# A Nyström attention and two-layer feed-forward kernel: the first stretch of the first layer written out as one fixed order for three engines

## The chip, the cores and the metric

The kernel runs on one core of a Trainium2 chip. The metric is device time in microseconds (us) of one execution. The kernel before took 865.08 us (median of three runs, 864.27 to 865.76).

## The reference, cut to what matters

Four images (batch entries) of 576 tokens go through Nyström attention with eight heads of width 64, then through two feed-forward layers.

```
q_lm, k_lm = block means of q, k over 18 tokens     # 32 landmarks
A  = softmax(q  @ k_lm.T * scale)                   # 576 x 32
Bm = softmax(q_lm @ k_lm.T * scale)                 # 32 x 32
C  = softmax(q_lm @ k.T * scale)                    # 32 x 576
Z  = Bm.T / (norm1(Bm) * norminf(Bm) + 1e-6)
for _ in range(6): Z = 2*Z - Z @ Bm @ Z
x  = A @ Z @ C @ v                                  # heads side by side: 2304 x 512
x  = ((x @ w_a) * (x @ w_b)) @ w_out                # first layer, 1536 wide
h  = x @ w_in;  out = (h * tanh(softplus(h))) @ w_out2   # second layer, 2048 wide, Mish
```

The weights arrive as 64-bit floats and are rebuilt as 32-bit ones on the chip.

## The kernel before, in words

**Attention of one image** is a list of steps: `kl` and `ql` (landmark sums on VectorE), `sB` and `BB` (the small softmax and its norms), six `NS` (the inverse), `sC0`, `sC1`, `ET0`, `ET1`, `U` (scores of the landmarks against k, their transposes, the product with v), `M` (inverse times U), and `A0`, `A1` with `A0n`, `A1n` (the left softmax in two halves of the tokens). Each step takes its PSUM from a pair of banks, tagged `at` or `bm`.

**Units** rebuild the weights. One unit is a DMA into a stage buffer (`stg`, three of them, and eight more at the start), an `Abs` on ScalarE (L317), and four VectorE instructions (L320 to L325). A unit of `w_out` has a split into a high and a low part as well (L334). Units 0 to 7 make `wab` of groups 0 and 1, units 8 to 11 four tiles `wo`, and so on up to 36.

**Folding** (`emit_bm`) multiplies `M` into `wab` and splits the result (`bm`). A **slot** (`emit_ab`) is then 12 matmuls into two banks `ps_ab`, a copy `ta` on ScalarE, a product `tg` on VectorE, and a split into `g` by ScalarE and GpSimd. Slots number 0 to 95, eight to a cell of one image and one third of the width: slots 0 to 7 are image 0, slots 8 to 15 image 1. An **output unit** (`emit_o1`) is 12 matmuls from four `g` and four `wo` into a bank `ps_o`, with an eviction into `x2acc`. `fill` issues matmuls of the identity that nobody reads.

**What sets the order.** Instructions of ScalarE and TensorE go through `Written` and keep the program's order as long as `Written.on` holds, which ends after step `A1` of image 0. Most of VectorE is free: a scheduler places its instructions by a simulated timeline. From slot 0 on a list `todo` says beside which slot each step of images 1 to 3 and each unit is emitted, and the scheduler orders the rest. SyncE issues all DMAs in one order, each when its buffer is free.

Before slot 56 the activation table for Mish is preloaded (L638); the exponentials of image 3 that come later load their own again.

Of the kernel before, what the change touches and what calls it, by code (L numbers as in the profile page):

```python
# [8 lines left out]
F32 = mybir.dt.float32  # L9
# [22 lines left out]
def nystrom_moe_kernel(ctx: ExitStack, tc: tile.TileContext, q, k, v, w_a, w_b, w_out1, w_in2, w_out2, out):  # L32
    nc = tc.nc
    NT = B * S
    ve, gp = nc.vector, nc.gpsimd

    class Written:
# [79 lines left out]

    def attention(ap, b, kt, qt, vt0=None):
# [3 lines left out]
        wheel = [0]  # L122
# [26 lines left out]
        def sB():  # L149
            p = pair()  # L150
            tile4(p, lambda o, rows, j: (o[:, 0:32], x["ql"][rows, j, :], x["kl"][rows, j, :]))
            st = x["st"] = sm([128, 2, 8], "stB")
            eb = sm([128, 2, LM], "eb")
            ve.tensor_reduce(out=st[:, :, 0], in_=p[:, :, 0:32], axis=AX, op=ALU.max)
            ve.tensor_tensor(eb, p[:, :, 0:32], st[:, :, 0:1].to_broadcast([128, 2, LM]), op=ALU.subtract)
            ac.activation(eb, eb, AF.Exp, scale=SC_B)
            ve.tensor_reduce(out=st[:, :, 2], in_=eb, axis=AX, op=ALU.add)
# [7 lines left out]
        def BB():  # L165

            st, bc = x["st"], x["bc"]
            p = pair()
            for c in range(2):
# [12 lines left out]
            ve.tensor_tensor(rz[:, :, 0], p[:, :, 64:96], rc, op=ALU.mult)  # L182
            ve.tensor_tensor(rz[:, :, 0], ist2, rz[:, :, 0], op=ALU.subtract)
            ve.tensor_tensor(rz[:, :, 1], bc[:, :, 0], rc, op=ALU.mult)
            x["n"] = 0

        def NS():
# [4 lines left out]
            p = pair()  # L192
            nx = x["rz"] = sm([128, 2, 2, LM], "rz", 2)
            for c in range(2):
                for h in range(4):
                    r = slice(32 * h, 32 * h + 32)
                    pe.matmul(
                        p[r, c, 32 * lo:64], rz[r, c, 0], rz[r, c, lo:2].rearrange("p a l -> p (a l)"),
                        start=True, stop=True,
                    )  # L200
            if not lo:
                ac.activation(nx[:, :, 0], p[:, :, 0:32], AF.Copy)
            ve.tensor_tensor(nx[:, :, 1], p[:, :, 32:64], rz[:, :, 1], op=ALU.add)
# [33 lines left out]
        def Uv():  # L237
            p = pair()
            for c in range(2):
                for i in range(5):  # L240
                    r = slice(0, min(128, S - 128 * i))
                    for j in range(4):
# [4 lines left out]
                        if (c, i, j) == (0, 0, 0):  # L247
                            tc.keep_in_program_order(ins)
# [6 lines left out]
        def M():  # L255
            p = pair()
            for c in range(2):
                pe.matmul(p[64 * c:64 * c + 64, 0, 0:128], x["U"][:, c], x["zd"][:, c].rearrange("p h l -> p (h l)"), start=True, stop=True)
            MT[b] = main.tile([128, 128], F32, tag="mt", bufs=3, name="mt")
            ac.activation(MT[b], p[:, 0, 0:128], AF.Copy)  # L260

        def A(r):
            p = pair()
# [3 lines left out]
            sa = x["sa"][:, r]  # L267
            for c in range(2):
                ve.transpose(out=sa[:, c], in_=p[:, c, 0:288])
            sa3 = sa.rearrange("p c (n l) -> p (c n) l", l=LM)  # L270
            ss = x["ss", r] = sm([128, 18, 4], "stA", 2)
            ve.tensor_reduce(out=ss[:, :, 0], in_=sa3, axis=AX, op=ALU.max)
            ve.tensor_tensor(sa3, sa3, ss[:, :, 0:1].to_broadcast([128, 18, LM]), op=ALU.subtract)
            ac.activation(sa, sa, AF.Exp, scale=SC_A)

        def An(r):
            ss, sa = x["ss", r], x["sa"][:, r]
            sa3 = sa.rearrange("p c (n l) -> p (c n) l", l=LM)
            ve.tensor_reduce(out=ss[:, :, 1], in_=sa3, axis=AX, op=ALU.add)
            ve.tensor_scalar(ss[:, :, 2], ss[:, :, 1], 1e-9, None, op0=ALU.add)  # L280
# [588 lines left out]
```

## Time and profile before

| | |
|---|---|
| median of three runs | 865.08 us |
| profiled execution, its own time | 862.38 us |
| its span, first to last instruction | 860.6 us |
| TensorE matmul busy | 805.4 us, 94% of the span |
| VectorE busy | 553.3 us, 64% |
| ScalarE busy | 346.1 us, 40% |
| GpSimd busy | 157.0 us, 18% |
| chain that ended last | PE 79%, DVE 12%, DMA 5% |

In the profile PE is TensorE's matmuls, DVE is VectorE, ACT is ScalarE, POOL is GpSimd, SP is SyncE. [...] A busy time is the time in which at least one instruction of the engine ran. The profiled run lies 2.7 us below the median.

### The profile page before, as it was taken

How to read it: one execution, taken by the hardware profiler on the slowest of the kernel's cores; microseconds unless marked ns; L12 is line 12 of the kernel's file. 1: busy time of each engine (PE TensorE's matmuls, PEld its weight loads, DVE VectorE, ACT ScalarE, POOL GpSimd, SP SyncE). 2: the span in 40 equal slices, each digit the busy share in tenths (PEclk: the TensorE clock that was granted, in tenths of full speed). 3: DMA queues.
4: the chain of work that ended last, by engine and by line, in shares of the span. 5: the costliest groups of instructions: out<-in, count | busy, mean ns of one | idle time of the engine just before them, and what ended most of it. 6: DMA issues, size and time to landing. Idle time of an engine off the chain costs nothing.

```text
span 860.6 us, 14629 instructions
## 1 busy us (share of the span) xinstructions
PE 805.4 (94%) x5830; PEld 696.0 (81%) x5830; DVE 553.3 (64%) x1024; ACT 346.1 (40%) x686; POOL 157.0 (18%) x147
## 2 busy tenths in 40 slices
PE   4767799999999999999898899999999999999998
PEld 3445578887897797887798799898989888998986
DVE  7787868888375379787996667858533347432433
ACT  3234436435332464353444545445323235332332
POOL 0022211222122133121226433521000000000000
PEclk9778699999999999999999999999999999999999
DMA  9532746649543816877576976789755446655502
GB/s 356 239 117 99 254 151 200 226 152 319 197 156 114 308 34 221 292 226 266 175 235 250 346 249 216 269 293 339 296 185 201 158 180 219 212 204 194 184 1 75
DMA packets 47605, 180.87 MB, mean 210 GB/s; under 512 B 4144, under 2 KB 12336, under 8 KB 37936
## 3 DMA queue, kind: packets, MB, share of 16 engines
q1 hardware_dynamic: 47536, 179.93, 58.8%
q8 instruction: 46, 0.75, 0.3%
q14 instruction: 23, 0.19, 0.1%
HBM read 126.44 MB, written 53.48 MB: 209 GB/s over the span
## 4 chain that ended last, share of the span: by engine, by line
PE 79%; DVE 12%; DMA 5%; issue 2%; ACT 1%; POOL 1%; SPq 0%; DVEq 0%; ACTq 0%
PE ps_ab L49 34%; PE ps_o L49 22%; PE ps_bm L49 13%; PE ps_at L49 10%; DVE f L324 1%; DMA wi2d<-f 1%; DVE f L325 1%; DVE f L320 1%; DMA qt<-in_q_dram 1%; DVE tg L437 1%; DMA kt<-in_k_dram 1%; DVE f L323 1%; DMA wo2d<-f 1%; DMA xq<-x2d 1%; DVE ql L138 1%
## 5 line engine op out<-in xcount | busy, mean ns | idle before, releaser
L49 PE MATMUL ps_ab<-xc,wc 128*128 128x384 f32 x1008 | 201.9, 339 | 2.6 <-ACT m L49 2.1
L49 PEld LDWEIGHTS ps_ab<-xc,wc 128*128 128x128 f32 x1008 | 181.6, 189 | 15.1 <-ACT m L49 2.3
L49 PE MATMUL ps_ab<-at,bm 128*128 128x288 f32 x1152 | 187.1, 303 | 6.9 <-DVE tg L437 4.3
L49 PEld LDWEIGHTS ps_ab<-at,bm 128*128 128x128 f32 x1152 | 161.3, 190 | 37.6 <-issue 9.8
L49 PE MATMUL ps_o<-g,wo 128*128 128x288 f32 x1152 | 182.2, 300 | 10.1 <-ACT wo L49 4.3
L49 PEld LDWEIGHTS ps_o<-g,wo 128*128 128x128 f32 x1152 | 162.6, 190 | 23.9 <-issue 7.3
L334 POOL TENSOR_TENSOR g<-tg,g 128x288 fp32r<-128x288 f32 x96 | 88.1, 918 | 283.6 <-ACT g L49 283.6
L49 ACT ACTIVATE m<-c 128x384 f32<-128x384 f32 x96 | 50.4, 525 | 185.5 <-DVE c L759 185.5
L49 PE MATMUL ps_bm<-wo,g 128*128 128x512 f32 x288 | 94.1, 394 | 0.3 <-ACT g L49 0.3
L49 PE MATMUL ps_at<-wo,g 128*128 128x512 f32 x288 | 83.3, 393 | 0.0
L49 PE MATMUL ps_o<-wo,g 128*128 128x512 f32 x288 | 79.4, 393 | 0.0
L49 ACT ACTIVATE g<-tg 128x288 fp32r<-128x288 f32 x96 | 42.6, 444 | 86.7 <-DVE tg L437 86.6
L334 DVE TENSOR_TENSOR g<-m,g 128x384 fp32r<-128x384 f32 x96 | 60.7, 633 | 25.8 <-ACT g L49 25.7
L437 DVE TENSOR_TENSOR tg<-ps_ab,ta 128x288 f32<-128x288 f32 x96 | 43.4, 452 | 30.3 <-PE ps_ab L49 24.3
L49 PEld LDWEIGHTS ps_at<-wo,g 128*128 128x128 f32 x288 | 53.9, 188 | 10.3
L49 PEld LDWEIGHTS ps_o<-wo,g 128*128 128x128 f32 x288 | 53.6, 188 | 8.9
L49 PEld LDWEIGHTS ps_bm<-wo,g 128*128 128x128 f32 x288 | 53.4, 187 | 7.0 <-ACT g L49 0.6
L49 ACT ACTIVATE ta<-ps_ab 128x288 f32<-128x288 f32 x96 | 38.9, 405 | 44.0 <-PE ps_ab L49 43.6
L49 ACT ACTIVATE g<-m 128x384 fp32r<-128x384 f32 x96 | 50.6, 527 | 2.9
L759 DVE TENSOR_TENSOR c<-ps_ab,m 128x384 f32<-128x384 f32 x24 | 13.4, 557 | 51.8 <-PE ps_ab L49 51.8
L49 PE MATMUL ps_bm<-wab,mt 64*32 64x512 f32 x384 | 42.2, 636 | 1.2 <-ACT mt L49 0.7
L759 DVE TENSOR_TENSOR u2s<-ps_ab,m 128x384 f32<-128x384 f32 x24 | 13.4, 557 | 44.6 <-PE ps_ab L49 44.2
(144 smaller groups left out, 832.8 us busy)
## 6 DMA issues: line engine op xcount, KB each, us to landing
wc<-wcd SPq DMA_DIRECT2D x16, 1792.0 KB, 7.3
wo<-wod SPq DMA_DIRECT2D x16, 1024.0 KB, 4.8
stg<-in_moe_w_out_dram SPq DMA_DIRECT2D x28, 512.0 KB, 4.5
wcd<-wc SPq DMA_DIRECT2D x8, 1792.0 KB, 7.2
wab<-wabd SPq DMA_DIRECT2D x10, 1024.0 KB, 6.5
stg<-in_moe_w_in_dram SPq DMA_DIRECT2D x16, 512.0 KB, 4.9
wod<-wo SPq DMA_DIRECT2D x8, 1024.0 KB, 6.5
stg<-in_moe_w_a_dram SPq DMA_DIRECT2D x12, 512.0 KB, 5.5
```

What stands on the lines that cost most here:

```text
L49: i = f(*a, **kw)
L138: i = ve.tensor_reduce(out=x[nm][:, j:j + 2], in_=src[:, j:j + 2].rearrange("p j (t k) -> p j t k", k=BLK), axis=AX, op=ALU.add,)
L320: i = ve.tensor_scalar(dst, dst, F32_TINY, F32_HUGE, op0=ALU.max, op1=ALU.min)
L323: ve.tensor_scalar(du, du, 3, 0x3FFFFFFF, op0=ALU.logical_shift_left, op1=ALU.bitwise_and)
L324: ve.scalar_tensor_tensor(du, hi, 0xC0000000, du, op0=ALU.bitwise_and, op1=ALU.bitwise_or)
L325: ve.scalar_tensor_tensor(du, lo, 29, du, op0=ALU.logical_shift_right, op1=ALU.bitwise_or)
L334: lo_eng.tensor_tensor(dst_lo, src, dst_hi.bitcast(F32), op=ALU.subtract)
L437: ve.tensor_tensor(tg, pb[:, 0:288], ta, op=ALU.mult)
L759: ve.tensor_tensor(t, p[:, 0:TB], other, op=ALU.add)
```

## The change

Image 0's and image 1's attention, units 0 to 19, the foldings of groups 0 and 1 for both images, slots 0 to 11 and the first eight output units are cut into pieces (Python generators, cut where the work passes to another engine). A table `ORDER_1` calls the pieces one by one, and VectorE's instructions, as those of ScalarE and TensorE, keep the order of the table. A plain name is a piece of image 0, `+` one of image 1, `c` a unit, `s` a slot, `f` and `F` foldings for image 0 and 1, `o` an output unit, a number so many fills. At `|` a third pair of PSUM banks (`p3`), which image 0's steps may use, becomes the two `ab` banks of the slots.

```
+    ac, pe, ve = Written(nc.scalar), Written(nc.tensor), Written(nc.vector)
...
+    ps3_ctx = ExitStack()
+    two = {"p3": ps3_ctx.enter_context(tc.tile_pool(name="ps3", bufs=1, space=PSUM, reuse_waits="tile"))}
...
+        out, step = [], 4 if b else 2
+        for src, nm, tag, bufs in ((k, "kt", "kv", 1), (q, "qt", "qt", 2)):
+            t = ap.tile([128, 4, S], F32, tag=tag, bufs=bufs, name=nm)
+            for j in range(0, 4, step):
+                nc.sync.dma_start(out=t[:, j:j + step].rearrange("p j s -> p (j s)"), in_=src[b][:, S * j:S * (j + step)])
...
+    PAIRS0 = {"sC0": "p3", "ET0": "bm", "ET1": "p3", "A0": "bm", "U": "p3"}
+    PAIRS1 = {"ET0": "bm", "ET1": "bm"}
...
-                        p[r, c, 32 * lo:64], rz[r, c, 0], rz[r, c, lo:2].rearrange("p a l -> p (a l)"),
+                        p[r, c, 32 * lo:64].rearrange("p (a l) -> p a l", l=LM), rz[r, 0, c], rz[r, lo:2, c],
...
-                ac.activation(nx[:, :, 0], p[:, :, 0:32], AF.Copy)
-            ve.tensor_tensor(nx[:, :, 1], p[:, :, 32:64], rz[:, :, 1], op=ALU.add)
+                ac.activation(nx[:, 0], p[:, :, 0:32], AF.Copy)
+                yield
+            ve.tensor_tensor(nx[:, 1], p[:, :, 32:64], rz[:, 1], op=ALU.add)
...
-                    (ve if first else gp).tensor_tensor(zd[:, c], bd3, nx[:, c, 1:2].to_broadcast([128, 4, LM]), op=ALU.mult)
+                    (ve if b < 2 else gp).tensor_tensor(zd[:, c], bd3, nx[:, 1, c:c + 1].to_broadcast([128, 4, LM]), op=ALU.mult)
...
-            gp.tensor_tensor(at[:, 1], af, at[:, 0].bitcast(F32), op=ALU.subtract)
+            (ve if (b, r) == (0, 0) else gp).tensor_tensor(at[:, 1], af, at[:, 0].bitcast(F32), op=ALU.subtract)
...
+    N_UNITS, N_SLOTS = 20, 12
+    ORDER_1 = """
+        kl kl ql ql c0 sB sC0 sB c0 sB sC1 4 c1 sB sC0 BB 2 c2 sC1 BB c3 sC1 NS 2 c1 sC1 c2 c3 sC1 c0 c1 NS
...
-    u0.prefetch()
-    run0 = attention(ap, 0, kt, qt, load_v(ap, 0))
+    u0.prefetch(4)
+    vt0 = load_v(ap, 0)
+    u0.prefetch(8)
+    run0 = attention(ap, 0, kt, qt, vt0)
+    run1 = attention(ap, 1, *load_qk(ap, 1))
+    u0.prefetch(11)
...
-    for e in 'kl ql sB sC0 sC1 u 7 BB 8 NS ET0 1 NS ET1 u NS 2 A0 NS u 2 A0n NS U u 3 NS 2 M u'.split():
...
+    def unit(n):
+        yield from u0.units[n][2](u0.st[n])
+        u0.n = n + 1
+        if n > 7:
+            u0.prefetch(3)
...
+    def go(text):
+        for e in text.split():
+            if e.isdigit():
+                fill(int(e))
+            elif e == "|":
+                ps3_ctx.close()
+                two["ab"] = ctx.enter_context(tc.tile_pool(name="psab", bufs=1, space=PSUM, reuse_waits="tile"))
+            elif e[0] == "+":
+                run1(e[1:], False)
+            elif e in part:
+                next(part[e], None)
+            else:
+                run0(e, False)
+
+    go(ORDER_1)
     Written.on = False
...
-            tc.keep_in_program_order(ac.engine.preload_act_table_set("mish"))
...
+        if si == 92:
+            held(ac.engine.preload_act_table_set("mish"))
```

On VectorE, where image 0's norms (`stB` from `ps_at`) become the first `rz` of the inverse, there stood before:

```order
L176 TENSOR_REDUCE stB<-ps_at 128x2x2
L325 SCALAR_TENSOR_TENSOR wab<-stg,wab 128x2x256
L177 TENSOR_TENSOR stB<-stB 128x2
L320 TENSOR_SCALAR wab<-wab 128x2x256
L178 TENSOR_SCALAR stB<-stB 128x2
L320 TENSOR_SCALAR wab<-wab 128x2x256
L323 TENSOR_SCALAR wab<-wab 128x2x256
L179 RECIPROCAL stB<-stB 128x2
L323 TENSOR_SCALAR wab<-wab 128x2x256
L324 SCALAR_TENSOR_TENSOR wab<-stg,wab 128x2x256
L182 TENSOR_TENSOR rz<-ps_at,stB 128x2x32
```

The same place now, in the changed program's line numbers (L56 is the wrapper, L378 a unit's clamp):

```order
L56 TENSOR_REDUCE stC<-ps_bm 128x2
L56 TENSOR_REDUCE stB<-ps_at 128x2x2
L56 TENSOR_TENSOR stB<-stB 128x2
L56 TENSOR_SCALAR stB<-stB 128x2
L56 RECIPROCAL stB<-stB 128x2
L56 TENSOR_TENSOR rz<-ps_at,stB 128x64
L56 TENSOR_TENSOR rz<-ist,rz 128x64
L56 TENSOR_TENSOR rz<-bc,stB 128x64
L56 TENSOR_TENSOR stC<-stC 128x2
L56 TENSOR_SCALAR stC<-stC 128x2
L378 TENSOR_SCALAR wab<-wab 128x2x256 x3
```

The units' instructions (`wab`) that stood between the steps of the norm stand behind them.

On TensorE, from the first folding of image 0 (`ps_bm<-wab,mt`) to the second, there stood before:

```order
L49 MATMUL ps_bm<-wab,mt 32x512 x8
L49 MATMUL ps_at<-qt,kl 32x288 x8
L49 MATMUL ps_ab<-at,bm 128x288 x24
L49 MATMUL ps_at<-kl,ql 32x32 x2
L49 MATMUL ps_bm<-kt,ql 32x288 x2
L49 MATMUL ps_at<-kl,ql 32x32 x6
L49 MATMUL ps_bm<-kt,ql 32x288 x6
L49 MATMUL ps_at<-kt,ql 32x288 x8
L49 MATMUL ps_ab<-at,bm 128x288 x12
L49 MATMUL ps_at<-bc,ones 32x64 x4
```

And now, from the first folding up to image 1's first norm:

```order
L56 MATMUL ps_bm<-wab,mt 32x512 x8
L56 MATMUL ps_ab<-at,bm 128x288 x18
L56 MATMUL ps_at<-kt,ql 32x288 x8
L56 MATMUL ps_bm<-kt,ql 32x288 x8
L56 MATMUL ps_ab<-at,bm 128x288 x6
L56 MATMUL ps_at<-kl,ql 32x32 x8
L56 MATMUL ps_bm<-ident,E 128x128 x4
L56 MATMUL ps_bm<-ident,E 64x128
L56 MATMUL ps_ab<-at,bm 128x288 x6
L56 MATMUL ps_bm<-ident,E 128x128 x4
L56 MATMUL ps_bm<-ident,E 64x128
L56 MATMUL ps_at<-bc,ones 32x64 x4
```

Two slots (24 matmuls `ps_ab<-at,bm`) and then image 1 became halves of slots between image 1's steps; image 1's transposes moved ahead of its norms, and the output units behind slot 8.

On SyncE, around the loads of units 11 to 14 (`stg`), there stands now:

```order
L109 DMA kt<-in_k_dram 128x2304
L427 DMA wabd_84<-wab 128x2048
L364 DMA stg<-in_moe_w_out_dram 128x1024
L364 DMA stg<-in_moe_w_a_dram 128x2x512
L459 DMA wo1d_89<-wo_682 128x1024
L459 DMA wo1d_90<-wo_847 128x1024
L109 DMA qt<-in_q_dram 128x2304
L364 DMA stg<-in_moe_w_b_dram 128x2x512
L459 DMA wo1d_92<-wo_965 128x1024
L364 DMA stg<-in_moe_w_a_dram 128x2x512
```

The `qt` here is image 3's; it waits for the buffer of image 1's q, which step `A1` of image 1 reads last, and three more stage loads queue behind it. Before, the `qt` in the same place was image 2's.

## Rows read from the trace of the kernel before

**Rows 1.** Stretch, length, busy (count) of PE, PEld, DVE, ACT, POOL, clock, DMA, GB/s.

```profile
0.00:44.20 44.20, 25.44 (x380) 18.41 (x380) 31.02 (x77) 13.40 (x27) 2.73 (x13) 0.85 0.74 289
...
0.00:122.00 122.00, 85.68 (x986) 62.73 (x989) 90.65 (x197) 44.82 (x96) 19.14 (x29) 0.82 0.58 210
...
122.00:302.00 180.00, 175.87 (x1648) 147.90 (x1646) 123.00 (x248) 74.64 (x163) 41.60 (x47) 0.99 0.58 203
...
302.00:481.00 179.00, 168.86 (x1348) 148.62 (x1347) 143.65 (x259) 82.64 (x167) 53.93 (x52) 1.00 0.65 220
```

**Rows 2.** What VectorE waited for from 44.2 to 122: total, times, longest.

```profile
DVE bm L334 <- ACT bm L49: 6.0, 3, 3.1
```

**Rows 3.** VectorE in order of time: start, length, line, operation [idle before].

```profile
6.03 2.61 DVE L138 TENSOR_REDUCE kl<-kt 128x64 f32<-128x1152 f32 x2 [4.15 <-DMA kt<-in_k_dram]
...
8.82 2.61 DVE L138 TENSOR_REDUCE ql<-qt 128x64 f32<-128x1152 f32 x2 [0.18 <-DMA qt<-in_q_dram]
...
19.01 0.28 DVE L176 TENSOR_REDUCE stB<-ps_at 128x4 f32<-128x128 f32 x1
...
23.76 0.22 DVE L183 TENSOR_TENSOR rz<-ist,rz 128x64 f32<-128x64 f32 x1
...
62.54 0.28 DVE L176 TENSOR_REDUCE stB<-ps_at 128x4 f32<-128x128 f32 x1
...
63.98 0.21 DVE L183 TENSOR_TENSOR rz<-ist,rz 128x64 f32<-128x64 f32 x1
```

**Rows 4.** TensorE in order of time: the first matmuls of slots 0, 8 and the last of 11.

```profile
44.23 0.79 PE L49 MATMUL ps_ab<-at,bm 128*128 128x288 f32 x4 [0.69 <-ACT bm L49]
...
101.33 0.69 PE L49 MATMUL ps_ab<-at,bm 128*128 128x288 f32 x4
...
120.76 1.05 PE L49 MATMUL ps_ab<-at,bm 128*128 128x288 f32 x6
```

**Rows 5.** VectorE's forms from 0 to 121.8: count, busy, mean ns, idle before.

```profile
L273 DVE TENSOR_TENSOR sa<-sa,stA 128x576 f32<-128x576 f32 x4 | 3.0, 752 | 0.1
...
L207 DVE TENSOR_TENSOR zd<-bdm,rz 128x128 f32<-128x128 f32 x2 | 0.5, 289 | 0.1
```

**Rows 6.** ScalarE around the table loads of 302 us.

```profile
302.59 1.28 ACT L638 ACT_TABLE_LOAD   x1
...
303.89 0.45 ACT L49 ACTIVATE g<-tg 128x288 fp32r<-128x288 f32 x1
...
304.35 1.28 ACT L49 ACT_TABLE_LOAD   x1
```

**Rows 7.** ScalarE at the start of the second layer.

```profile
481.37 1.28 ACT L49 ACT_TABLE_LOAD   x1
```

**Rows 8.** TensorE near slot 92.

```profile
456.46 1.33 PE L49 MATMUL ps_ab<-at,bm 128*128 128x288 f32 x8 [1.38 <-DVE tg L437]
```

**Rows 9.** TensorE at one inverse step of image 1.

```profile
79.52 0.43 PE L49 MATMUL ps_at<-rz 32*32 32x64 f32 x16
```

**Rows 10.** ScalarE at that step.

```profile
80.08 0.23 ACT L49 ACTIVATE rz<-ps_at 128x64 f32<-128x64 f32 x1 [1.32 <-PE ps_at L49]
```

**Rows 11.** VectorE at that step.

```profile
80.34 0.22 DVE L203 TENSOR_TENSOR rz<-ps_at,rz 128x64 f32<-128x64 f32 x1 [0.20 <-ACT rz L49]
```

**Rows 12.** Two stretches of 20 us, columns as in Rows 1.

```profile
60.00:80.00 20.00, 17.50 (x215) 13.89 (x215) 13.44 (x31) 11.52 (x28) 5.47 (x6) 0.91 0.28 96
...
80.00:100.00 20.00, 11.06 (x157) 5.67 (x158) 15.76 (x37) 6.81 (x14) 4.47 (x4) 0.52 0.68 246
```

**Rows 13.** TensorE: image 1's A0 and A1.

```profile
76.34 0.72 PE L49 MATMUL ps_at<-qt,kl 64*32 64x288 f32 x16 [0.76 <-DVE rz L203]
...
84.00 1.22 PE L49 MATMUL ps_at<-qt,kl 64*32 64x288 f32 x16 [2.81 <-DVE rz L203]
```

**Rows 14.** DMA issues from 75 to 125: count, size, median us to landing.

```profile
stg<-in_moe_w_a_dram SPq DMA_DIRECT2D x4, 512.0 KB, 3.7
```

**Rows 15.** What the DMA queue waited for, 44 to 125.

```profile
SPq L307 <- DVE wab L325: 24.1, 6, 6.1
```

More of the change, by code (lines that the diff above doesn't have):

```diff
@@ L34, in nystrom_moe_kernel, with held @@
     NT = B * S
-    ve, gp = nc.vector, nc.gpsimd
+    gp = nc.gpsimd
+    last = [None]
+    def held(i):
+        if last[0] is not i:
+            last[0] = i
+            tc.keep_in_program_order(i)
     class Written:
@@ L121, in attention, with pair @@
         first = b == 0
-        wheel = [0]
+        tags = {0: PAIRS0, 1: PAIRS1}.get(b, {})
         def sm(shape, nm, bufs=1, tag=None):
             return ap.tile(shape, F32, tag=tag or nm, bufs=bufs, name=nm)
-        def pair():
-            wheel[0] += 1
-            return pair_bank("bm" if first and wheel[0] % 2 else "at")
+        def pair(step):
+            return pair_bank(tags.get(step, "at"))
         def lm_sum(src, nm):
@@ L167, in BB @@
             st, bc = x["st"], x["bc"]
-            p = pair()
+            p = pair("BB")
             for c in range(2):
@@ L228, in e_T @@
                 x["ET"] = sm([128, 2, 5, 128], "ET")
-            p = pair()
+            p = pair("ET%d" % c)
             for i in range(5):
@@ L237, in Uv @@
         def Uv():
-            p = pair()
+            p = pair("U")
             for c in range(2):
@@ L351, in step @@
                     self.prefetch()
-                    self.units[self.n - 1][2](self.st[self.n - 1])
+                    for _ in self.units[self.n - 1][2](self.st[self.n - 1]):
+                        pass
                     self.prefetch()
@@ L383, in split_unit @@
             f3 = f
-        to_f32(f, st)
-        split(dst_hi, dst_lo, f3, ac, gp if u0.n == 36 else ve)
+        yield from to_f32(f, st)
+        yield
+        ac.activation(dst_hi, f3, AF.Copy)
+        yield
+        (gp if u0.n == 36 else ve).tensor_tensor(dst_lo, f3, dst_hi.bitcast(F32), op=ALU.subtract)
     wo1 = {}
@@ L413, in emit_bm @@
         t = main.tile([128, 2, 2, 512], F32R, tag="bm", bufs=3, name="bm")
-        split(t[:, 0], t[:, 1], p, ac, ve)
+        yield
+        ac.activation(t[:, 0], p, AF.Copy)
+        yield
+        ve.tensor_tensor(t[:, 1], p, t[:, 0].bitcast(F32), op=ALU.subtract)
         bm[b, g] = t
+    def emit_bm(b, g):
+        for _ in fold(b, g):
+            pass
     g1 = {}
@@ L459, in emit_o1, with evict @@
             return
[L460 to L469 removed]
+        def evict():
+            if o1n.setdefault((b, hf), 0) == 0:
+                x2acc[b, hf] = main.tile([128, 4, 288], F32, tag="x2", bufs=4, name="x2acc")
+            dst = x2acc[b, hf][:, d]
+            o1n[b, hf] += 1
+            if o1n[b, hf] <= 4:
+                ac.activation(dst, p[:, 0:288], AF.Copy)
+            else:
+                ve.tensor_tensor(dst, p[:, 0:288], dst, op=ALU.add)
+            if o1n[b, hf] == 12:
+                nc.sync.dma_start(out=x2d[b][:, :, 288 * hf:288 * hf + 288], in_=x2acc[b, hf])
+        if not now:
+            return evict
+        evict()
     wi2d = [dram.tile([128, 4, 256], F32, name=f"wi2d{n}") for n in range(8)]
@@ L611, in nystrom_moe_kernel @@
     slots = [(b, w, *((y, x) if (b, w) == (0, 0) else (x, y)), ch) for b, w in CELLS for x in range(2) for y in range(2) for ch in range(2)]
-    o1q, todo, runs = [], [], {}
+    o1q, runs = [(1, 0, 0, d) for d in range(4)], {1: run1}
     def load(b):
@@ L657, in between @@
                     o1q.pop(0)
-            if si in (7, 8) and i == 1:
-                for part in range(2):
-                    emit_o1(*o1q[0], part)
-                o1q.pop(0)
-        emit_ab(b, 2 * w + gi, hf, ch, between)
-        if si == 1:
-            emit_bm(0, 1)
-        if ks in (5, 7) and ci + 1 < len(CELLS):
+        for i, _ in enumerate(ab(b, 2 * w + gi, hf, ch)):
+            if i == 1:
+                between(0)
+        between(1)
+        if ci > 0 and ks in (5, 7) and ci + 1 < len(CELLS):
             nb, nw = CELLS[ci + 1]
```

174 lines of the change are left out of this document (106 added, 68 removed).

## The prediction

> **What bounds the kernel now.** I read the stretches first. From 122 us on TensorE is busy 175.87 of 180 us and 168.86 of 179 [rows 1]: what is done there is TensorE's own work, and an order cannot shorten it much. In the first 122 us it is busy only 85.68 us, at a mean clock of 0.82 [rows 1]. This is where time can be had: 36 us of idle TensorE, and some more in matmuls at the lower clock. The reader is to see next that VectorE has the most to do there after TensorE: 90.65 busy us of 122 [rows 1], where ScalarE has 44.82. VectorE's idle time is 13.2 us up to 44.2 us (44.20 less 31.02) and 18.2 us from there to 122 (77.8 less 59.6, both differences of two rows). The longest wait of the second stretch is for ScalarE's half of a split, 6.0 us in three waits [rows 2].
>
> The order of time shows why TensorE stands. Image 0's norms take from 19.01 to the end of the subtraction at 23.98, that is 4.97 us; image 1's same steps take 62.54 to 64.19, 1.65 us [rows 3]. Between the former stand the units' instructions that the order shows. TensorE comes to slot 0 at 44.23 and to slot 8, the first of image 1, only at 101.33 [rows 4]; until then it did image 1's small steps one by one.
>
> **The point to compare.** The table ends with slot 11 and eight output units. Just ahead of its slot 12 the changed TensorE has issued 12 slots, 8.75 output units (one is 12 matmuls) and the foldings of five groups. Before, the last half of slot 11 starts at 120.76 [rows 4]; by its end at 121.8 there were 12 slots, 8.5 output units and a third of the fifth folding. The missing three matmuls and half folding are some 0.9 us, less what the order there had already begun, so I take 122 us as the same point. What the changed kernel needs to reach it is the whole question; behind it the order is nearly the old one.
>
> **The parts and their cost.**
>
> *The fixed order.* The sum goes by VectorE, since both kernels have rebuilt units 0 to 17 there, and the same attention. Work: 90.65 us as before [rows 1]. Two operations come over from GpSimd: the low half of image 0's first `at` (128x576, as the subtraction of that size with 752 ns) and image 1's two `zd` (289 ns each overlapping, 0.5 together) [rows 5]: 1.25 us. Together 91.9 us.
>
> To this comes idle time that the new order leaves. First stretch: q and k arrive in halves. Before, VectorE waits 4.15 us for k, then 0.18 for q; each sum of both halves takes 2.61 [rows 3]. With halves the first half sum (1.3 us) runs while the second half is on its way, and VectorE is through `ql` about 1.3 us earlier: of 13.2 idle us the opening keeps 4.5. The chain behind it has short waits for TensorE and ScalarE, each with one unit instruction to fill it; I give it 1.5 us. So 6 us, between 5 and 13.2 (all of the old).
>
> Second stretch: at the least one stall that I can name. Image 1's `BB`, `U` and first inverse step take the one pair `at` in turn, and VectorE has two unit instructions for cover; from a U of 20 to 40 small matmuls I estimate 3 us, and 1 us for a stage load that comes late. So 4 at the least and 18.2 at the most, what the old order left. I take 10, about half way, because the splits' waits for ScalarE remain (the largest cause of before) while the written order places unit work beside them.
>
> Sum: 91.9 + 6 + 10 = 107.9 us, against 122: 14.1 us gained. Best 91.9 + 5 + 4 = 100.9 (21.1 gained); worst 91.9 + 13.2 + 18.2 = 123.3 (1.3 lost). TensorE can follow: from slot 8 it needs 20.5 us before (101.33 to 121.8, all busy) and now 1.67 output units more there, as these are put off: some 2.7 us more. So slot 8 must start by about 84.7 us, 17 us earlier than before, and slot 0 near 36 (8 us earlier, which the 3.3 us of the norms, the 1.3 us of the halves and the further unit work behind the chain give).
>
> *Halves kept apart.* ScalarE writes one half of an inverse step's result, VectorE the other. TensorE's step of 79.52 ends at 79.95 [rows 9]; ScalarE copies from 80.08 to 80.31 [rows 10], and VectorE starts only at 80.34, released by ScalarE [rows 11]. Where the halves lie in separate addresses, VectorE can start at 80.08: 0.26 us a step, five steps an image. In image 0 and 1 this is in the sum above (it is part of the idle time, at most 2.6 us); in images 2 and 3 the dense TensorE hides it. Nothing further, bounds 0 and 0.5.
>
> *The Mish table.* Behind the first load at the start there are three: at 302.59 and 304.35 [rows 6], with one copy between, and at 481.37 [rows 7]; one at slot 92 takes their place. Each is 1.28 us of ScalarE. TensorE shows no idle at either place that the load ended, and goes on with output units: gain 0, at most 1.3. That of slot 92 comes where TensorE already stands for VectorE's product, 1.38 us at 456.46 [rows 8], and that product needs a copy `ta` of ScalarE. There the load is not covered if it falls just ahead of a `ta`: 0 to 1.3 us lost; I take 0.6.
>
> *Behind slot 12.* Units 20 to 35 stay spread as before, VectorE is at 123 of 180 us there [rows 1], so nothing stops the shift; bounds 1 us either way.
>
> Total: 14.1 - 0.6 = 13.5 us. The profiled execution took 862.38 us, its span 860.6 and 1.8 around it: it would become 848.9. It lay 2.7 us under the median of the runs shown, 865.08; from that the forecast is 851.6.
>
> **Rivals.**
>
> *A. TensorE's clock falls and its small steps become the chain.* With the output units put off, TensorE's work between slots 0 and 8 lies thin. [...]
>
> *B. The written order stalls on a late stage load, and the kernel becomes slower.* SyncE issues in order. Image 3's q stands ahead of unit 13's load and waits for image 1's `A1`, and unit 13 to 17 stand on VectorE, now in fixed order, ahead of image 1's second half of `A` and so ahead of slot 12. Stage loads already waited 24.1 us for VectorE in six waits before [rows 15]. A load lands 3.7 us after its issue [rows 14], and ScalarE and VectorE add 3 us a unit. In my order `A1` of image 1 runs near 84 us, where it ran before too (84.00 [rows 13]). Each us later moves slot 12 by one. It decides from `A1` at 98 us on; at 104 slot 12 comes at 128: 865.1 + 6 = 871. Against it: A1 needs only image 1's `A0` out of its banks and three slots, some 10 us behind `M`.
>
> *C. The order gains in front and loses it behind*, since the eight output units wait together and slot 12 finds VectorE in arrears with products and foldings. The dense TensorE for 20 us speaks for it, VectorE's 68% from 122 to 302 us [rows 1] against. Time 865, no change.
>
> *D. It goes better:* idle time near its lower bound, 18 us gained: 847.
>
> **Chances.** Forecast, 9 to 17 us gained, 0.60; A 0.18; B 0.07; C 0.04; D 0.11. The range has to leave out B, C and the ends of A and D: 846 to 860. What a measurement of this kernel can tell from no change is about 0.2%, 1.7 us: faster 0.89 (forecast, A, D), the same 0.04, slower 0.07.
>
> **What would show it.** In the changed profile: slot 0 on TensorE near 36 us instead of 44.23, slot 8 near 85 to 88 instead of 101.33, the end of slot 11 near 108 instead of 121.8; VectorE's idle time up to there some 16 us; inverse steps with VectorE beside ScalarE and no wait between; two table loads in all. From slot 12 to the end the same length within 2 us. I am wrong if slot 0 comes early but slot 8 does not (B or A, told apart by the clock of 36 to 85 us and by waits of ScalarE for `stg`), or if slot 12 comes early and the rest grows by as much (C).

## The result, and the profile after

The changed kernel takes 854.66 us (median; 852.74 to 855.78), the kernel before in the same comparison 864.67 (863.96 to 865.76): a ratio of 0.9881, 95% interval 0.9859 to 0.9902, 10.0 us less. The profiled execution took 852.74 us with a span of 850.7, against 862.38 and 860.6.

The stretches of the kernel after, up to the point that the prediction compares (from, to, length, then busy us and instructions of PE, PEld, DVE, ACT and POOL, granted clock as a share of the full one, DMA share, GB/s):

```profile
0.00:36.80 36.80, 19.72 (x353) 13.09 (x353) 27.71 (x65) 12.99 (x27) 1.32 (x12) 0.88 0.97 376
36.80:87.70 50.90, 34.48 (x449) 24.49 (x450) 47.37 (x100) 20.80 (x46) 10.29 (x10) 0.84 0.44 161
87.70:111.00 23.30, 23.30 (x168) 21.30 (x168) 22.75 (x40) 11.66 (x25) 5.78 (x5) 0.96 0.59 183
0.00:111.00 111.00, 77.51 (x968) 58.88 (x969) 97.83 (x202) 45.45 (x97) 17.39 (x27) 0.88 0.65 237
```

They answer to [rows 1]. VectorE (third pair) now stands idle for 3.5 us between 36.8 and 87.7, and for 13.2 of the first 111; before it was 31.4 of 122. From 87.7 to 111 TensorE is busy throughout (23.30 of 23.30 us) and VectorE nearly so (22.75): from there on the sum by VectorE alone no longer says what bounds. The clock did not fall: 0.88 up to 111 us, where it was 0.82 up to 122.

TensorE in order of time, kernel after (start, duration, tile written and read, count, idle time before it and what ended that):

```profile
15.72 0.42 PE L56 MATMUL ps_at<-rz 32*32 32x64 f32 x16 [1.55 <-DVE stC L56]
...
33.78 0.40 PE L56 MATMUL ps_ab<-at,bm 128*128 128x288 f32 x1 [1.77 <-ACT at L56]
36.87 4.45 PE L56 MATMUL ps_ab<-at,bm 128*128 128x288 f32 x17 [2.69 <-DVE at L56]
...
48.66 0.36 PE L56 MATMUL ps_at<-kl,ql 64*32 64x32 f32 x16 [4.82 <-ACT E L56]
...
84.92 1.96 PE L56 MATMUL ps_bm<-wab,mt 64*32 64x512 f32 x16 [5.69 <-DVE bm L56]
86.81 3.94 PE L56 MATMUL ps_ab<-at,bm 128*128 128x288 f32 x18
...
111.04 1.62 PE L56 MATMUL ps_ab<-at,bm 128*128 128x288 f32 x11
```

Against [rows 4]: slot 0 runs from 36.87 (its first matmul stands alone at 33.78) instead of 44.23, slot 8 from 86.81 instead of 101.33, and slot 12 follows 8.75 output units at 111.0 (11 of its 12 matmuls; one stands ahead, at 108.02), where the point of equal work was 122, which the prediction estimated. Slot 11 ends earlier, near 100.7, and the output units that were put off follow it; the prediction put its end near 108, at the point of equal work. The first step of the inverse, which started at 24.12 before, is at 15.72. So 11.0 us are gained by slot 12, and 1.1 given back behind it (739.7 against 738.6 us to the end).

VectorE at image 0's norms, kernel after; this answers to [rows 3]:

```profile
14.04 0.28 DVE L56 TENSOR_REDUCE stB<-ps_at 128x4 f32<-128x128 f32 x1
14.35 0.16 DVE L56 TENSOR_TENSOR stB<-stB 128x2 f32<-128x2 f32 x1
...
15.21 0.23 DVE L56 TENSOR_TENSOR rz<-ist,rz 128x64 f32<-128x64 f32 x1
```

1.4 us from the reduction to the end of the subtraction instead of 4.97: no unit's instruction stands between.

### The profile page after: what moved, and what is told of

It is laid out like the page before. It is cut to its first block, busy times and chain, and to the rows that moved or that the text cites. A ratio compares the mean times of both kernels' runs of the same rounds, so it can differ in the third digit from the quotient of the medians.

```text
span 850.7 us, 14559 instructions
## 1 busy us (share of the span) xinstructions
PE 794.7 (93%) x5802; PEld 691.9 (81%) x5802; DVE 565.8 (67%) x1027; ACT 342.1 (40%) x684; POOL 153.2 (18%) x144
## 4 chain that ended last, share of the span: by engine, by line
PE 75%; DVE 14%; DMA 6%; issue 3%; ACT 2%; SPq 0%; POOL 0%; ACTq 0%; DVEq 0%
PE ps_ab L56 33%; PE ps_o L56 21%; PE ps_bm L56 11%; PE ps_at L56 10%; DVE f L56 5%; DMA kt<-in_k_dram 3%; DMA wi2d<-f 2%; DVE tg L56 1%; DVE f L378 1%; DVE bm L56 1%; DMA wo2d<-f 1%; DVE kl L56 1%; ACT f L374 1%; DVE x2acc L56 1%; DVE s L56 1%
## 5 line engine op out<-in xcount | busy, mean ns | idle before, releaser
L56 PE MATMUL ps_ab<-xc,wc 128*128 128x384 f32 x1008 | 201.7, 340 | 4.8 <-DVE u2s L56 3.1
L56 PE MATMUL ps_ab<-at,bm 128*128 128x288 f32 x1152 | 192.0, 307 | 13.4 <-DVE tg L56 6.9
L56 PEld LDWEIGHTS ps_ab<-at,bm 128*128 128x128 f32 x1152 | 165.4, 194 | 41.9 <-issue 11.8
L56 PEld LDWEIGHTS ps_ab<-xc,wc 128*128 128x128 f32 x1008 | 181.8, 189 | 16.9 <-DVE u2s L56 3.4
L56 PE MATMUL ps_o<-g,wo 128*128 128x288 f32 x1152 | 180.0, 298 | 3.1 <-DVE x2acc L56 2.1
L56 PEld LDWEIGHTS ps_o<-g,wo 128*128 128x128 f32 x1152 | 161.0, 188 | 15.4 <-issue 5.9
L56 ACT ACTIVATE m<-c 128x384 f32<-128x384 f32 x96 | 50.2, 523 | 189.6 <-DVE c L56 189.5
L56 PE MATMUL ps_bm<-wo,g 128*128 128x512 f32 x288 | 95.5, 396 | 0.3 <-ACT g L56 0.3
L56 PE MATMUL ps_at<-wo,g 128*128 128x512 f32 x288 | 82.9, 395 | 0.0
L56 DVE TENSOR_TENSOR g<-m,g 128x384 fp32r<-128x384 f32 x96 | 66.7, 696 | 23.0 <-ACT g L56 23.0
L56 PE MATMUL ps_o<-wo,g 128*128 128x512 f32 x288 | 79.6, 393 | 0.0
L56 ACT ACTIVATE g<-tg 128x288 fp32r<-128x288 f32 x96 | 42.4, 442 | 79.9 <-DVE tg L56 79.7
L56 DVE SCALAR_TENSOR_TENSOR f<-stg,f 128x512 uint32<-128x512 uint32 x88 | 72.1, 823 | 1.6
L56 PEld LDWEIGHTS ps_at<-wo,g 128*128 128x128 f32 x288 | 54.3, 189 | 10.7
L56 DVE TENSOR_TENSOR tg<-ps_ab,ta 128x288 f32<-128x288 f32 x96 | 43.2, 451 | 29.7 <-PE ps_ab L56 21.9
L56 ACT ACTIVATE ta<-ps_ab 128x288 f32<-128x288 f32 x96 | 38.9, 405 | 57.4 <-PE ps_ab L56 56.9
L56 PEld LDWEIGHTS ps_o<-wo,g 128*128 128x128 f32 x288 | 53.6, 188 | 9.1
L56 PEld LDWEIGHTS ps_bm<-wo,g 128*128 128x128 f32 x288 | 53.7, 189 | 7.0 <-ACT g L56 0.6
L56 ACT ACTIVATE g<-m 128x384 fp32r<-128x384 f32 x96 | 50.3, 523 | 2.6
L56 DVE TENSOR_TENSOR c<-ps_ab,m 128x384 f32<-128x384 f32 x24 | 13.4, 557 | 50.6 <-PE ps_ab L56 50.6
L56 PE MATMUL ps_bm<-wab,mt 64*32 64x512 f32 x384 | 39.3, 644 | 6.2 <-DVE bm L56 6.2
```

## The experiments

All twelve were timed beside the kernel before, which lay at 862.5 to 863.4 us on those chips; the ratio is to it. "Slot 8" is the start of its first matmul, "layer 2" the start of the 12 matmuls behind `u2s` (the first sum on VectorE in the second layer that TensorE waits for), both on TensorE in the profiled execution. The two columns ahead of the ratio are that execution's span and its part behind "layer 2".

| kernel | slot 8 | layer 2 | span | behind layer 2 | ratio, 95% |
|---|---|---|---|---|---|
| before | 101.3 | 480.5 | 860.6 | 380.1 | 1 |
| after | 86.8 | 469.5 | 850.7 | 381.2 | 0.9881 [0.9859, 0.9902] |
| e4_ve_free | 98.7 | 484.1 | 866.1 | 382.0 | 1.0063 [1.0039, 1.0087] |
| e9_small_only | 103.6 | 487.4 | 868.4 | 381.0 | 1.0056 [1.0035, 1.0077] |
| e2_halves | 87.2 | 470.4 | 851.9 | 381.5 | 0.9898 [0.9863, 0.9934] |
| e3_whole | 87.6 | 467.0 | 848.7 | 381.7 | 0.9886 [0.9854, 0.9918] |
| e1_mish56 | 87.2 | 477.5 | 858.2 | 380.7 | 0.9923 [0.9894, 0.9952] |
| e11_mish72 | 87.4 | 467.8 | 848.7 | 380.9 | 0.9846 [0.9826, 0.9866] |
| e12_mish40 | 86.1 | 466.2 | 846.9 | 380.7 | 0.9872 [0.9837, 0.9907] |
| e5_pool_light | 86.1 | 466.7 | 847.8 | 381.1 | 0.9851 [0.9815, 0.9887] |
| e6_wo0_ve | 86.9 | 464.2 | 849.1 | 384.9 | 0.9886 [0.9851, 0.9921] |
| e7_order2 | 88.6 | 468.6 | 849.4 | 380.8 | 0.9879 [0.9837, 0.9921] |
| e8_kt_first | 84.8 | 467.5 | 848.8 | 381.3 | 0.9888 [0.9847, 0.9928] |
| e10_all | 86.7 | 466.9 | 851.4 | 384.5 | 0.9868 [0.9847, 0.9889] |

**VectorE free again, under the same table.** ScalarE and TensorE keep the order of `ORDER_1`, VectorE's instructions are left to the scheduler:

```
         on = True
+        free = None
...
-                if Written.on:
+                if Written.on and self is not Written.free:
...
+    Written.free = ve
```

> The changed kernel with the table's order kept for TensorE and ScalarE alone; the scheduler places VectorE's instructions in the same stretch. Theory (VectorE's written order is the main part): 4 to 9 us more, 859 to 864; image 0's norms to its first inverse step again take over 3 us and slot 0 starts after 40. Rival (the order on TensorE and ScalarE and the smaller pieces do it, and VectorE follows): within 2 us of 854.7.

Measured: 868.14 us, 1.0063: slower than before, and more than the 859 to 864 that were expected. VectorE, then TensorE of this kernel (columns as above):

```profile
19.18 0.28 DVE L57 TENSOR_REDUCE stB<-ps_at 128x4 f32<-128x128 f32 x1
19.39 1.88 DVE L57 SCALAR_TENSOR_TENSOR wab<-stg,wab 128x512 uint32<-128x512 uint32 x3
21.19 0.15 DVE L57 TENSOR_TENSOR stB<-stB 128x2 f32<-128x2 f32 x1
...
22.53 0.22 DVE L57 TENSOR_TENSOR rz<-ist,rz 128x64 f32<-128x64 f32 x1
```

```profile
22.90 0.65 PE L57 MATMUL ps_at<-rz 32*32 32x64 f32 x16 [6.63 <-DVE rz L57]
...
98.67 0.61 PE L57 MATMUL ps_ab<-at,bm 128*128 128x288 f32 x1 [8.23 <-ACT at L57]
```

The unit's three instructions are back inside the norm, TensorE waits 6.63 us for the first inverse step and 8.23 for image 1's `at`. Slot 8 loses 11.9 of its 14.5 us again (98.7 against 86.8) with VectorE's freedom alone. It then starts 2.6 us earlier than before and still reaches layer 2 3.6 us later (484.1 against 480.5); what costs these 6.2 us in between was not followed. The written order of the other two engines, without VectorE's, costs time. The converse, VectorE's written order with the other two engines as before, was not run.

**The small edits without the table.** The kernel before, with the halves apart, q and k of image 0 in two transfers, and the Mish load at slot 92:

```
-            nc.sync.dma_start(out=t.rearrange("p j s -> p (j s)"), in_=src[b])
+            step = 4 if b else 2
+            for j in range(0, 4, step):
+                nc.sync.dma_start(out=t[:, j:j + step]..., in_=src[b][:, S * j:S * (j + step)])
...
-                ac.activation(nx[:, :, 0], p[:, :, 0:32], AF.Copy)
-            ve.tensor_tensor(nx[:, :, 1], p[:, :, 32:64], rz[:, :, 1], op=ALU.add)
+                ac.activation(nx[:, 0], p[:, :, 0:32], AF.Copy)
+            ve.tensor_tensor(nx[:, 1], p[:, :, 32:64], rz[:, 1], op=ALU.add)
...
-            tc.keep_in_program_order(ac.engine.preload_act_table_set("mish"))
...
+        if si == 92:
+            tc.keep_in_program_order(ac.engine.preload_act_table_set("mish"))
```

> The kernel before with the three small edits of the change and without the written order: halves of the inverse's steps apart, q and k of the first image in two transfers, the Mish table loaded at slot 92. Theory (the written order is the whole gain, the small edits lie beside TensorE's work): 862.5 us within 1.5, slot 8 near 101 and slot 12 near 122 as before. Rival (the run with the load at slot 56 gave back 4 us of the gain, so the load's new place is worth that by itself): near 858.5, with the front of the kernel as before and the gain between 300 and 480 us of the span. Second rival (the small edits help only where VectorE follows the written order): 862 to 863 with up to 1 us earlier at slot 0.

Measured: 868.02 us, 1.0056; none of the three expectations held. TensorE:

```profile
18.21 0.43 PE L49 MATMUL ps_at<-bc,ones 32*32 32x64 f32 x8 [4.18 <-ACT E L49]
...
46.40 0.79 PE L49 MATMUL ps_ab<-at,bm 128*128 128x288 f32 x4 [0.53 <-ACT bm L49]
```

TensorE's first wait, for `kl`, is 1.4 us shorter (7.4 us, before 8.8), but the matmuls of image 0's norm then wait 4.18 us, put down to ScalarE's `E`, where they waited 2.3 before; slots 0 and 8 come 2.2 us later, the way from slot 8 to layer 2 takes 4.7 more and the part behind it another 0.9. So the small edits by themselves are no part of the gain; with a scheduler free to lay VectorE out anew around them, the kernel takes 4.8 us more (7.8 in the profiled execution). Which of the three does it was not separated.

**The halves and the transfers, each undone in the changed kernel.** The first lays `rz` out as before (`rz[:, :, 0]` for `rz[:, 0]` and so on), the second is

```
-        out, step = [], 4 if b else 2
+        out, step = [], 4
```

> The changed kernel, but with the two halves of an inverse step interleaved in memory as before, so that VectorE again waits for ScalarE in each step. Theory (VectorE's amount of work sets slot 12, and its idle time there is short): at most 1.3 us more, 854.7 to 856; the wait of VectorE for ScalarE's rz grows from 1.5 to about 3 us in the first 111 us. Rival (the chain of inverse steps is the path): 0.26 us in each of ten steps and again in images 2 and 3, 857.5.

> The changed kernel, but image 0's q and k come in whole transfers again. Theory: VectorE is through ql 1.2 us later and everything up to slot 12 with it: 856, slot 12 at 112.2. Rival (hidden by later waits, as that for image 1's k at 33.7): no change, 854.7.

Measured: 0.9898 and 0.9886, neither to be told from 0.9881. With the halves interleaved VectorE's waits for ScalarE's `rz` came to 1.1 us up to 111 us instead of the 3 expected (1.5 in the kernel after); with whole transfers slot 8 comes 0.8 us later and the span is 2.0 us shorter. Why the halves do nothing is seen at the second and third step of the inverse, first in the kernel after, then with the halves interleaved again (ScalarE's copy, VectorE's sum):

```profile
17.50 0.24 ACT L56 ACTIVATE rz<-ps_at 128x64 f32<-128x64 f32 x1
17.77 0.23 DVE L56 TENSOR_TENSOR rz<-ps_at,rz 128x64 f32<-128x64 f32 x1 [0.25 <-ACT rz L56]
...
19.41 0.21 ACT L56 ACTIVATE rz<-ps_at 128x64 f32<-128x64 f32 x1
19.66 0.23 DVE L56 TENSOR_TENSOR rz<-ps_at,rz 128x64 f32<-128x64 f32 x1 [0.39 <-ACT rz L56]
```

```profile
17.55 0.24 ACT L56 ACTIVATE rz<-ps_at 128x64 f32<-128x64 f32 x1
17.82 0.22 DVE L56 TENSOR_TENSOR rz<-ps_at,rz 128x64 f32<-128x64 f32 x1 [0.25 <-ACT rz L56]
```

VectorE starts 0.25 to 0.27 us behind ScalarE's start in both, 0.03 to 0.04 us after the copy ends: in these runs separate addresses for the results did not let the two run side by side. Both engines read the same `ps_at` and write one tile `rz`; which of the two holds VectorE back no run separates. Reading from separate banks was not tried.

**The Mish load put elsewhere.** At slot 56 as before (e1), at 72 (e11), at 40 (e12), each with a second load for the tables that it displaced and a third in front of Mish:

```
-        if si == 92:
+        if si == 72:
             held(ac.engine.preload_act_table_set("mish"))
```

> The changed kernel, but with the Mish table loaded at slot 56 again, so that the exponentials and the second layer load their tables as before: three loads after the first instead of one, 2 x 1.28 us more of ScalarE. My theory (the loads were never on TensorE's path): the time stays at 854.7 within 1 us; the start of slot 12 stays at 111.0. Rival (the table is a part of the gain): 2 to 2.6 us more, 857.

> The changed kernel with the Mish load issued at slot 72 in the program, which the scheduler lets float up to right behind the written order, ahead of the second attention's softmax: three later loads, as in the run with the load at slot 56, but at another place and with another order of the instructions behind it. If what cost 4 us there is the pair of loads by itself (2 x 1.28 us of ScalarE, in front of a softmax that TensorE comes to wait for), here again 855 to 857. If it was the order that the scheduler chose behind that place, this order is another draw: anything from 850 to 859, and its waits for ta on ScalarE (7.9 us there, 1.7 in the changed kernel, between 290 and 455 us) say which.

> The changed kernel with the Mish load at slot 40, near 200 us, ahead of four softmax steps on ScalarE: again three later loads, and a pair of them straight in front of a softmax as in the run with slot 56. (The run with slot 72 had its pair at 363 and 370 us, behind the last softmax, and lost nothing.) If a pair in front of a softmax is what costs 4 us, because VectorE and then TensorE come to wait for it: 855 to 857 us here, with an idle VectorE of about 2 us before the reduction behind that softmax. If the pair is hidden and the 4 us were the order that the scheduler laid out behind slot 56: another draw, between 849 and 858; of the kernels so far the part behind slot 12 took 737 to 747 us, whatever was edited in front, and 738 to 740 is the likeliest, so 849 to 853.

Measured: 856.4 us (850.44 to 859.93), 850.79 and 851.03. In the run with slot 72 the description of the place was wrong: the pair ran at 363.45 and 369.69, behind the last softmax, not ahead of it. The run with slot 40 is the one that puts a load straight in front of a softmax; its ScalarE, then its VectorE:

```profile
226.03 1.28 ACT L56 ACT_TABLE_LOAD   x1
227.33 0.69 ACT L56 ACTIVATE sa<-sa 128x576 f32<-128x576 f32 x1
```

```profile
228.05 0.76 DVE L56 TENSOR_REDUCE stA<-sa 128x18 f32<-128x576 f32 x1 [1.84 <-ACT sa L56]
```

VectorE waits 1.84 us for it, TensorE has slots and output units to do and waits for nothing of it. So three loads instead of one cost nothing that was measured at these two places. With slot 56 the ratio is 0.0042 above that of the kernel after, some 3.6 us, but the two intervals overlap, so that this difference is not certain. The profiled execution, the slowest of the eight of this kernel, is 7.5 us longer, and what it lost stands elsewhere. ScalarE and TensorE of that run, 100 us behind its loads:

```profile
389.05 0.66 ACT L374 ACTIVATE f<-stg 128x512 f32<-128x512 f32 x1 [5.78 <-DMA wi2d<-f]
389.61 0.43 ACT L56 ACTIVATE g<-tg 128x288 fp32r<-128x288 f32 x1
...
389.95 0.39 ACT L56 ACTIVATE ta<-ps_ab 128x288 f32<-128x288 f32 x1
```

```profile
390.39 0.85 PE L56 MATMUL ps_ab<-at,bm 128*128 128x288 f32 x2 [3.60 <-ACT ta L56]
```

A unit's copy into `f` waits for the transfer that empties an earlier `f` (`wi2d<-f`), and the `ta` queued behind it on ScalarE holds TensorE: 7.9 us in five waits for `ta` between 290 and 455 us, where the kernel after has 1.7. Moving the load made the scheduler lay ScalarE out anew, and in this order such copies stand ahead of a `ta`. These 6.2 us more are most of the 7.5 of this one execution, and fit a spread of 9.5 us over its runs; what else belongs to the difference was not tested.

**GpSimd lightened.** In slots 0 to 11 it writes zeros in place of the low halves:

```
-        gp.tensor_tensor(t[:, 1], tg, t[:, 0].bitcast(F32), op=ALU.subtract)
+        if Written.on:
+            gp.memset(t[:, 1].bitcast(F32), 0.0)
+        else:
+            gp.tensor_tensor(t[:, 1], tg, t[:, 0].bitcast(F32), op=ALU.subtract)
```

> The changed kernel, where GpSimd writes zeros into the low halves of the products of slots 0 to 11 instead of subtracting (those low halves are left out). Theory (VectorE's instructions are stretched while GpSimd subtracts): the units' SCALAR_TENSOR_TENSOR fall from a mean of 794 ns to about 700 up to slot 12, VectorE's busy time there from 97.8 to about 95, and slot 12 starts near 108.5; 852.5. Rival (the longer work is only the moved operations): the means stay, 854.7.

Measured: 848.66 us, 0.9851. VectorE's groups of the unit's last step up to 111 us (count, then busy us and mean ns), kernel before up to 122, after, and this one:

```profile
L324 DVE SCALAR_TENSOR_TENSOR wab<-stg,wab 128x512 uint32<-128x512 uint32 x13 | 9.4, 727 | 0.2
L325 DVE SCALAR_TENSOR_TENSOR wab<-stg,wab 128x512 uint32<-128x512 uint32 x13 | 8.9, 690 | 0.1
```

```profile
L56 DVE SCALAR_TENSOR_TENSOR wab<-stg,wab 128x512 uint32<-128x512 uint32 x27 | 20.2, 761 | 0.2
L56 DVE SCALAR_TENSOR_TENSOR f<-stg,f 128x512 uint32<-128x512 uint32 x8 | 7.6, 952 | 0.2
```

```profile
L56 DVE SCALAR_TENSOR_TENSOR wab<-stg,wab 128x512 uint32<-128x512 uint32 x28 | 20.1, 729 | 0.2
L56 DVE SCALAR_TENSOR_TENSOR f<-stg,f 128x512 uint32<-128x512 uint32 x8 | 6.2, 774 | 0.2
```

With GpSimd busy 9.0 instead of 17.4 us, the same instruction takes 729 and 774 ns instead of 761 and 952. It saves 2.3 us of durations (27 by 32 ns and 8 by 178), and slots 8 and 12 come 0.7 and 0.6 us earlier (slot 12 at 110.4, where 108.5 was expected). So GpSimd stretches VectorE's instructions; how much of the span that is worth lies between the 0.7 us in front and the 2.6 us between the two ratios, whose intervals overlap.

**Three waits taken away, alone and together.** The low half of layer 2's first `wo` on VectorE (e6), the last third of the table rearranged (e7), image 1's k ahead in the transfer queue (e8), and all three (e10). The edit of e6, and of e8 its core:

```
-        split(t[:, :, 0], t[:, :, 1], f, ac, gp)
+        split(t[:, :, 0], t[:, :, 1], f, ac, ve if k == 0 else gp)
...
+                if b == 1:
+                    tc.keep_in_program_order(d)
```

> The changed kernel, where the low half of the second layer's first wo tile is subtracted on VectorE and not on GpSimd (2.61 us at 466). Theory (that GpSimd operation holds VectorE's weight sum for 2.1 us, and so the first u2s, for which TensorE stands 3.06 us): the wait falls under 1.5 us, 853. Rival (u2s is late for another reason): no change or later, since VectorE has 1 us more to do.

> The changed kernel with the last third of the table in another order: unit 10's last instructions and the low half of image 1's first folding ahead of image 1's A0n, the first output units in TensorE's hole from 79 to 85, units 15 to 17 behind A1n. Theory (up to 86 us VectorE bounds, from there to slot 12 TensorE, so work moved from the dense stretch into the hole is gained): slot 12 starts 2 to 4 us earlier, 851 to 853. Rival (slot 12 hangs on A1n on VectorE alone, and that gets later by unit 10): no change.

> The changed kernel with image 1's k ahead of its q and of units 8 to 10 in the DMA queue. Theory: VectorE's wait of 1.56 us for that k at 33.7 goes, slot 0 and all up to slot 12 come 1 to 1.5 us earlier, 853.3. Rival (k then holds the queue up while it waits for its buffer, or the time is lost again by slot 12): no change.

> The changed kernel with the three edits that each measured 0.8 to 1.0 us under it: the last third of the written order rearranged, the first wo low half of the second layer on VectorE instead of GpSimd, the second image's k ahead in the transfer queue. If they are three separate waits, their gains add: 852.4 - 3 = 849.5 us. If they are within the scatter of a kernel whose runs lie 1.5 us either side, or if two of them shorten the same wait, 851 to 852. Slot 0's run of matmuls should start near 35 and not 36.9 us in any case, from the earlier k.

Measured: 0.9886, 0.9879, 0.9888 and together 0.9868: the gains that the profiles show do not add up to one that the runs show. The clearest is e6. GpSimd, VectorE and TensorE of the kernel after at the start of layer 2:

```profile
466.08 2.61 POOL L395 TENSOR_TENSOR wo<-s_out,wo 128x1024 fp32r<-128x1024 f32 x1 [8.41 <-ACT wo L56]
466.40 2.56 DVE L56 TENSOR_TENSOR s<-s_in 128x256 f32<-128x256 f32 x1
...
469.49 3.89 PE L56 MATMUL ps_ab<-xc,wc 128*128 128x384 f32 x11 [3.06 <-DVE u2s L56]
```

and TensorE of e6:

```profile
464.20 1.31 PE L56 MATMUL ps_ab<-xc,wc 128*128 128x384 f32 x6 [0.91 <-DVE u2s L56]
465.80 1.31 PE L56 MATMUL ps_ab<-xc,wc 128*128 128x384 f32 x6 [0.29 <-DVE c L56]
469.54 1.22 PE L56 MATMUL ps_bm<-wo,g 128*128 128x512 f32 x2 [2.43 <-ACT g L56]
```

The wait for `u2s` falls from 3.06 to 0.91 us, and the next step then waits 2.43 for a `g`, and the part behind "layer 2" is 3.7 us longer: the wait became another wait. ScalarE shows why:

```profile
466.63 1.06 ACT L56 ACTIVATE wo<-s_out 128x1024 fp32r<-128x1024 f32 x1 [3.78 <-DMA s_out<-wo2d]
```

This copy waits 3.78 us for a transfer, and ScalarE's steps that make the `g` stand behind it; they end at 469.48. In the kernel after the same copy waits 3.58 us and that `g` ends at 472.44, 1.06 us before TensorE comes to it at 473.50. So of the 3.06 us no more than 1.06 could be had as long as ScalarE keeps this order. In e8 the wait of VectorE for image 1's k is gone (1.56 us at 33.66 in the kernel after), slot 8 comes 2.0 us earlier, and the span is 1.9 shorter, which its timed runs do not show apart from their scatter. In e7 another 2.98 us wait for `bm` stands at 82.71 in place of the 5.69 at 84.92, and slot 8 comes 1.8 us later. All three edits together (e10) have slot 0's run of matmuls at 35.1 instead of 36.9, as expected, and not the 849.5 us that a sum of three gains would give, but 852.27.

## Why the prediction was right, and where its terms were not

Forecast 13.5 us, measured 10.0, in the profiled pair 9.6.

*The mechanism holds.* The first 122 us were bound by the order on VectorE: the table brought slot 8 forward by 14.5 us, and freeing VectorE again took 11.9 of these away. TensorE's clock (rival A) was 0.84 between 36.8 and 87.7; before, the same work from slot 0 to slot 8 had 0.73:

```profile
44.20:101.30 57.10, 39.54 (x454) 26.84 (x455) 45.95 (x97) 22.43 (x49) 13.47 (x13) 0.73 0.45 160
```

About as many matmuls (449, before 454) thus stood in a shorter stretch and at a higher clock, the opposite of rival A. What sets the clock no run separates, so none shows how low it would fall in thinner work, on which rival A's chance of 0.18 rested; the traces show 0.91 where TensorE was busy 17.50 of 20 us before and 0.52 where it was 11.06 [rows 12], and the 0.84 of after, with 34.48 of 50.9. Image 1's second `A` runs at 77.5 us, far from the 98 at which rival B decides.

*The step that was mis-sized is VectorE's work,* 91.9 in the sum and 97.8 in the trace; its idle time, 16 in the sum, came to 13.2. Their sum is 111.0 instead of 107.9, and these 3.1 us are most of what the forecast was too high. By durations the work grew by 6.0 us (7.2 in busy time, where overlapping instructions count once). Of that 1.3 are the operations that come from GpSimd, as predicted. 1.15 are the low half of the fifth folding, which the prediction counted on TensorE and not on VectorE. 3.65 are the units' last step: one instruction more (0.76), the rest the same instruction at 805 instead of 721 ns on the mean. The means of before come from the two rows of before that stand with e5 and these two:

```profile
L324 DVE SCALAR_TENSOR_TENSOR f<-stg,f 128x512 uint32<-128x512 uint32 x4 | 2.7, 684 | 0.0
L325 DVE SCALAR_TENSOR_TENSOR f<-stg,f 128x512 uint32<-128x512 uint32 x4 | 3.4, 841 | 0.1
```

The prediction took the duration from a trace in which VectorE and GpSimd met less often: 7 of 34 such instructions ran beside a `TENSOR_TENSOR` of GpSimd before and took 846 ns on the mean, 13 of 35 after and took 1009; the others took 688 and 685. With GpSimd lightened the mean falls from 805 to 739 ns, most of the way back. One place, VectorE and then GpSimd of the kernel after; alone, one such instruction takes 0.68 us:

```profile
85.06 2.55 DVE L56 SCALAR_TENSOR_TENSOR f<-stg,f 128x512 uint32<-128x512 uint32 x2
```

```profile
84.46 1.40 POOL L320 TENSOR_TENSOR at<-af,at 128x576 fp32r<-128x576 f32 x1 [4.79 <-ACT at L56]
85.82 1.24 POOL L519 TENSOR_TENSOR g<-tg,g 128x288 fp32r<-128x288 f32 x1
```

*The idle time came out near the sum by luck.* Up to 36.8 us it was 9.1 (6 in the sum), behind that 4.1 (10 in the sum, 4 the lower bound): two errors of opposite sign. In front the sum did not have the wait for image 1's k, 1.56 us. Behind, it kept VectorE's waits for ScalarE's half of a split, 6.0 us before, and they are gone:

```profile
L56 DVE TENSOR_TENSOR bm<-ps_bm,bm 128x1024 fp32r<-128x1024 f32 x5 | 6.0, 1209 | 0.0
```

The stall that it named came to 0.56 us at `U` and 0.89 at the first inverse step, not to 3 (the `U` of one image is 80 matmuls, not 20 to 40), and no wait for a late stage load is seen there. TensorE's part from slot 8 to slot 12 was 24.2 us and not 23.2: 27 more matmuls of output units stand there than before, where the prediction has 1.67 units, that is 20.

*Halves apart:* the step failed. VectorE still starts 0.25 to 0.27 us behind the start of ScalarE's copy, so nothing of the 2.6 us was had; the sum survives it because the idle time as a whole was rated 2.8 us too high.

*The Mish load:* predicted 0.6 lost, with two loads in all, and two there are. ScalarE of the kernel after:

```profile
441.21 1.28 ACT L761 ACT_TABLE_LOAD   x1
442.50 0.41 ACT L56 ACTIVATE ta<-ps_ab 128x288 f32<-128x288 f32 x1
```

It does fall just ahead of a `ta`, as in the bad case, and TensorE has output units to do meanwhile. The runs with three loads at slots 40 and 72 are as fast, so its number and place are worth nothing that was measured; the order that the scheduler lays out behind it may be worth several us, as the profile of the run with slot 56 suggests.

*Behind slot 12:* 1.1 us longer, within the 2 named as a sign and just beyond the 1 that the sum allowed. The rest of the first layer is 2.6 us shorter up to the wait that ends at 469.49 (355.4 from slot 12, before 358.0), that wait is 2.5 longer (3.06, before 0.54), and what follows 1.1 longer. Rival C was there in small.

## What to carry to other kernels

Where two engines follow a written order and a third, the busiest of the stretch, is laid out by a simulated timeline, write it out too: here the written order of the others without it took 868.14 us, a ratio of 1.0063. When work is packed tighter, take each duration at what it costs beside the neighbour that it will then meet, not at its mean in the loose trace: the instruction of the units' last step took 721 ns before and 805 after. A wait of 2 to 3 us removed at one place of a kernel in which most of the time is dense is worth what the timed runs show, not what its row shows: in e6 a wait of 3.06 us fell to 0.91, and the ratio was 0.9886 beside 0.9881.

## What the runs showed of the hardware

A VectorE instruction `s<-s_in` of 128x256 took 0.42 us in the kernel before, where it started 0.07 us ahead of GpSimd's subtraction at 479.66, and 2.56 us after, where it started 0.32 us behind one. VectorE and GpSimd of the kernel before, to be read against the two rows of after that stand with e6:

```profile
479.59 0.42 DVE L504 TENSOR_TENSOR s<-s_in 128x256 f32<-128x256 f32 x1
479.66 5.13 POOL L334 TENSOR_TENSOR wo<-s_out,wo 128x1024 fp32r<-128x1024 f32 x2 [10.31 <-ACT wo L49]
```

Where VectorE came later, 2.29 us of GpSimd's instruction were left when its own started, and it ended 0.27 behind it. Where VectorE came first, GpSimd's two instructions from 479.66 on took 5.13 us, 2.57 each, no more than the 2.61 of after. In e6, with GpSimd idle until 467.77, the same instruction took 0.42 us at 463.26. What in GpSimd's instruction lengthens VectorE's no run separates.
